# Longer rows for the windowed keys: four heads to a key tile, with row groups exchanged in the copies out of the transposes

## Chip, cores, metric

One core of one Trainium2 chip. The metric is the device time of one execution, in microseconds.

## The reference

Two attention blocks of one decode step, whose outputs stand side by side:

```python
# A: full attention.   B: the same, over the last W = 2048 positions only.
# 4 batches, 32 query heads, 8 key heads, 8192 positions, 128 elements a head, bf16
q = (x @ wq) -> [4, 32, 1, 128]
k = repeat(k_cache[:, :, Sk - W:, :], 4, axis=1)     # B; A takes the whole cache
v = repeat(v_cache[:, :, Sk - W:, :], 4, axis=1)
p = softmax(q @ k^T * 128 ** -0.5)
out = (p @ v) -> [4, 1, 4096] @ wo
```

Nearly all the bytes are keys and values: 134 MB of A, 33.6 MB of B, and 16.8 MB of weights.

## The kernel before

The work is cut into 20 units of 4 MB of keys and 4 MB of values. Units 0 to 3 are B, one batch each, all eight heads. Units 4 to 19 are A, two heads of one batch each. Keys and values each have two buffers of `[128 partitions, 128 token slots, 128]`. SyncE issues all the loads, in order, each behind the wait that its buffer is free.

```python
def kv_load(kind, u):                       # B units
    for q in range(NSEG):                   # NSEG = 4 pieces of 1 MB
        base = cache[un["b"], 2 * q, SK - W:SK, :]
        # TS = 32 tokens: rows of 8 KB; partition = 2 * run + head, two heads a piece
        src = bass.AP(..., ap=[[TS * DH, 64], [SK * DH, 2], [1, TS * DH]])
        w = [("T", tjob_idx[(u - 2, 4 * q + 3)])]       # keys: tile 4q+3 of the unit two before is transposed
        op("sp", dma(buf[:, slot, q * TS:(q + 1) * TS, :], src), waits=w, ...)
    # (A units: one DMA, [[NT * DH, 128], [1, NT * DH]], rows of 32 KB)

def pe_T(u, k):                             # tile k of 16: four transposes into one PSUM bank
    for pi in range(4):
        t0 = k * 8 + 2 * pi                 # two token slots each, as f32 pairs
        pe.transpose(out=bkf[:, pi * 128:(pi + 1) * 128], in_=K_sbf[:, slot, t0:t0 + 2, :], identity=identf)
    # copy PSUM -> SBUF: VectorE (as int32) for even k, ScalarE (as bf16) for odd k

def pe_S(u, k):                             # scores of tile k, three tiles after its transposes
    for pi in range(4):
        t = k * 8 + 2 * pi
        for e in range(2):                  # even and odd elements of the head
            pe.matmul(out=stb[:, t % NTH * C:(t % NTH + 2) * C], lhsT=ktv[:, pi, :, e],
                      rhs=RQc[:, u % 2, t // TS, e, :], start=(e == 0), stop=(e == 1))
```

A score row (one partition) gets columns for both heads of its piece; a mask by the partition's parity removes the wrong one. So exactly two heads may share a score tile, and the score of (partition, slot) must belong to the same token and head as the value at (partition, slot). That tied keys to the 8 KB rows of the values.

## Time and profile before

| | before |
|---|---|
| median of the first three runs | 440.12 us (439.64 to 440.31) |
| bytes, mean rate | 184.75 MB, 422 GB/s |
| rate while B loads / in the A stretch | 422 / 431 GB/s |
| busy: PE, DVE, ACT | 83%, 48%, 44% |

The page, the windows, the waits and two landings stand in the prediction. Two more views are needed to follow the change. The first is the page's list of transfers (KB each, median us from issue to landing):

```profile
K_sb<-in_B_k_cache_dram SPq DMA_DIRECT2D x16, 1024.0 KB, 22.0
V_sb<-in_B_v_cache_dram SPq DMA_DIRECT2D x16, 1024.0 KB, 18.4
```

A megabyte is 2.5 us of transfer at this rate, so of 22 us nearly 20 are time spent in the queue. The second is the groups of ScalarE and of VectorE by form between 34 and 124 us (count, busy us, mean ns, idle before), the copies out of the transposes:

```profile
L288 ACT ACTIVATE KT_sb<-KT 128x1024 bf16<-128x1024 bf16 x40 | 40.7, 1025 | 25.3 <-PE KT L279 25.3
L287 DVE COPY KT_sb<-KT 128x512 int32<-128x512 int32 x40 | 27.6, 690 | 36.8 <-PE KT L279 36.5
```

ScalarE waits 25.3 us for PE beside 40.7 of copying, VectorE 36.5 beside 27.6; in the same window no wait of PE for either of them is listed, so neither holds PE up.

### The profile page before, as it was taken

How to read it: one execution, taken by the hardware profiler on the slowest of the kernel's cores; microseconds unless marked ns; L12 is line 12 of the kernel's file. 1: busy time of each engine (PE TensorE's matmuls, PEld its weight loads, DVE VectorE, ACT ScalarE, POOL GpSimd, SP SyncE). 2: the span in 40 equal slices, each digit the busy share in tenths (PEclk: the TensorE clock that was granted, in tenths of full speed). 3: DMA queues.
4: the chain of work that ended last, by engine and by line, in shares of the span. 5: the costliest groups of instructions: out<-in, count | busy, mean ns of one | idle time of the engine just before them, and what ended most of it. 6: DMA issues, size and time to landing. Idle time of an engine off the chain costs nothing.

```text
span 437.9 us, 15510 instructions
## 1 busy us (share of the span) xinstructions
PE 363.9 (83%) x7174; PEld 336.5 (77%) x7184; DVE 209.5 (48%) x404; ACT 193.3 (44%) x217; POOL 29.1 (7%) x96
## 2 busy tenths in 40 slices
PE   0078898998998959896989598969878895989986
PEld 0068897997997959795979588968868795979975
DVE  0004455664565634463456247625644563556641
ACT  1033473563653625372635264534534361635630
POOL 7110000000000000000000000000100000000000
PEclk9999999999999997999899699989998999999999
DMA  8999999999999999999999999999999999999996
GB/s 336 431 412 418 419 419 419 421 445 406 450 431 431 417 445 431 434 428 431 434 434 428 432 434 431 428 434 431 406 456 431 431 428 434 431 431 410 446 407 253
DMA packets 12500, 184.75 MB, mean 422 GB/s; under 512 B 1428, under 2 KB 2504, under 8 KB 2760
## 3 DMA queue, kind: packets, MB, share of 16 engines
q1 hardware_dynamic: 12400, 184.56, 99.2%
q8 instruction: 8, 0.13, 0.1%
q14 instruction: 4, 0.03, 0.0%
q0 software_dynamic: 64, 0.02, 0.0%
q10 hardware_dynamic: 24, 0.01, 0.0%
HBM read 184.56 MB, written 0.01 MB: 421 GB/s over the span
## 4 chain that ended last, share of the span: by engine, by line
PE 51%; DMA 43%; issue 2%; DVE 1%; SPq 1%; PEld 1%; PEldq 0%
DMA K_sb<-in_A_k_cache_dram 29%; PE KT L279 25%; PE OT L326 10%; DMA K_sb<-in_B_k_cache_dram 7%; DMA V_sb<-in_A_v_cache_dram 7%; PE SB L310 4%; PE SA L310 4%; PE KT L384 4%; SPq L568 1%; PE SA L338 1%; DVE oacc L392 1%; PE KT L326 1%; PEld OT L326 1%; PE KT L262 0%; DVE OS L489 0%
## 5 line engine op out<-in xcount | busy, mean ns | idle before, releaser
L279 PE MATMUL KT<-identf,K_sb 128*128 128x128 f32 x1280 | 206.2, 294 | 44.0 <-DMA K_sb<-in_A_k_cache_dram 33.0
L288 ACT ACTIVATE KT_sb<-KT 128x1024 bf16<-128x1024 bf16 x160 | 163.4, 1025 | 121.1 <-PE KT L279 121.1
L279 PEld LDWEIGHTS KT<-identf,K_sb 128*128 128x128 f32 x1280 | 146.2, 148 | 49.4 <-DMA K_sb<-in_A_k_cache_dram 34.2
L287 DVE COPY KT_sb<-KT 128x512 int32<-128x512 int32 x160 | 110.5, 690 | 131.2 <-PE KT L279 129.9
L326 PE MATMUL OT<-PT,V_sb 128*128 128x64 bf16 x2560 | 78.1, 193 | 2.5 <-issue 1.4
L326 PEld LDWEIGHTS OT<-PT,V_sb 128*128 128x128 bf16 x2560 | 75.9, 98 | 2.7 <-issue 1.5
L457 ACT ACTIVATE PT<-Dt 128x512 bf16<-128x512 f32 x40 | 24.6, 632 | 84.1 <-DVE Dt L446 84.1
L310 PEld LDWEIGHTS SA<-RQc,KT_sb 128*128 128x128 bf16 x1280 | 56.7, 98 | 2.3
L310 PEld LDWEIGHTS SB<-RQc,KT_sb 128*128 128x128 bf16 x1280 | 51.1, 97 | 7.9 <-issue 4.4
L310 PE MATMUL SA<-RQc,KT_sb 128*128 128x16 bf16 x1280 | 56.2, 170 | 0.0
L310 PE MATMUL SB<-RQc,KT_sb 128*128 128x16 bf16 x1280 | 52.8, 170 | 0.0
L408 DVE TENSOR_REDUCE M<-SB 128x8 f32<-128x512 f32 (+1 forms) x20 | 13.8, 692 | 49.9 <-PE SB L310 49.9
L429 POOL PARTITION_ALL_REDUCE MB<-M1m x20 | 7.7, 387 | 333.3 <-DVE M1m L422 333.3
L384 PE MATMUL KT<-Wo_sb,OL 128*4 128x512 bf16 x80 | 18.9, 379 | 0.0
L200 PE MATMUL KT<-ident,x_sb 4*128 4x4 bf16 x8 | 0.6, 170 | 21.1 <-POOL identf L540 21.1
L200 PEld LDWEIGHTS KT<-ident,x_sb 4*128 4x128 bf16 x8 | 0.4, 113 | 21.3 <-issue 21.3
L464 DVE TENSOR_REDUCE LB<-SA 128x8 f32<-128x512 f32 (+1 forms) x20 | 13.7, 684 | 2.8 <-PE SA L338 2.8
L446 DVE TENSOR_TENSOR Dt<-SA,MBm 128x512 f32<-128x512 f32 x20 | 13.8, 692 | 0.7
L355 DVE TENSOR_TENSOR ORx<-KT,MSK 32x1024 bf16<-32x1024 bf16 x10 | 12.1, 1211 | 3.7 <-PE KT L350 3.7
L408 DVE TENSOR_REDUCE M<-SA 128x8 f32<-128x512 f32 (+1 forms) x20 | 13.6, 681 | 0.0
L446 DVE TENSOR_TENSOR Dt<-SB,MBm 128x512 f32<-128x512 f32 x20 | 13.6, 681 | 0.0
L338 PE MATMUL SA<-PT,onesb 128*128 128x128 bf16 x168 | 12.7, 218 | 0.0
(74 smaller groups left out, 119.7 us busy)
## 6 DMA issues: line engine op xcount, KB each, us to landing
K_sb<-in_A_k_cache_dram SPq DMA_DIRECT2D x15, 4096.0 KB, 22.6
V_sb<-in_A_v_cache_dram SPq DMA_DIRECT2D x15, 4096.0 KB, 30.6
K_sb<-in_B_k_cache_dram SPq DMA_DIRECT2D x16, 1024.0 KB, 22.0
V_sb<-in_B_v_cache_dram SPq DMA_DIRECT2D x16, 1024.0 KB, 18.4
V_sb<-in_B_wq_dram SPq DMA_DIRECT2D x1, 4096.0 KB, 12.5
V_sb<-in_A_wq_dram SPq DMA_DIRECT2D x1, 4096.0 KB, 22.0
Wo_sb<-in_B_wo_dram SPq DMA_DIRECT2D x4, 1024.0 KB, 11.9
K_sb<-in_A_k_cache_dram SPq DMA_DIRECT2D x2, 2048.0 KB, 18.9
```

What stands on the lines that cost most here:

```text
L279: ins = pe.transpose(out=bkf[:, pi * 128:(pi + 1) * 128], in_=K_sbf[:, slot, t0:t0 + 2, :].rearrange("p t d -> p (t d)"), identity=identf[ ...
L287: return e.tensor_copy(out=KT_sb.bitcast(I32)[:, tj % NKT, :], in_=bkf.bitcast(I32)[:, :])
L288: return e.activation(out=KT_sb[:, tj % NKT, :], in_=bk[:, :], func=ACTF.Copy)
L310: ins = pe.matmul(out=stb[:, t % NTH * C:(t % NTH + 2) * C], lhsT=ktv[:, pi, :, e], rhs=RQc[:, u % 2, t // TS, e, :], start=(e == 0), stop ...
L326: ins = pe.matmul(out=otb[:, s * NW:s * NW + w], lhsT=V_sb[:, slot, t, :], rhs=PT[:, slot, t * C:t * C + w], start=(j == 0), stop=(j == n ...
L338: ins = pe.matmul(out=SA[u % 2][:, s * NM:(s + 1) * NM], lhsT=onesb[:, :], rhs=PT[:, u % 2, c0:c0 + NM], start=(i == 0), stop=(i == n - 1))
L355: return dve.tensor_tensor(out=ORx[:, :, :, :], in0=bk[0:NR, 0:128].rearrange("p (i o r) -> p r o i", o=1, r=C).broadcast_to([NR, C, C, 12 ...
L384: ins = pe.matmul(out=bk[0:Bn, 0:D], lhsT=OL[:, i, :], rhs=Wo_sb[:, i, :], start=(i == 0), stop=(i == C - 1))
L408: return dve.tensor_reduce(out=M1[:, h * n:(h + 1) * n].rearrange("p (s h) -> p s h", h=C), in_=bank[:, :].rearrange("p (s j h) -> p s h j ...
L446: return dve.tensor_tensor(out=Dt[:, h * NTH * C:(h + 1) * NTH * C].rearrange("p (s j h) -> p s j h", s=Sh, h=C), in0=bank[:, :].rearrange ...
L457: return act.activation(out=PT[:, u % 2, a:b], in_=Dt[:, a:b], func=ACTF.Exp, scale=scale)
L464: return dve.tensor_reduce(out=LB[:, 0:n].rearrange("p (s h) -> p s h", h=C), in_=SA[u % 2][:, 0:NSEG * NM].rearrange("p (s j h) -> p s h ...
```

## The change

The intent: keys of B in rows of 16 KB, so in half as many packets. A row of 16 KB is 64 tokens, a piece then has 32 runs of four heads, and the transposed tile holds four heads. The copy out of PSUM, which the kernel before has too, exchanges groups of rows so that each score tile again holds two heads, in the layout of the values.

```diff
+    NPART = {"K": 2, "V": NSEG}
+        def tok0(k, pi):
+            return NTH * (k // (NJ // 2)) + TS * (pi // 2) + 4 * (k % (NJ // 2)) + 2 * (pi % 2)
 # pe_T and pe_S
-                    t0 = k * 8 + 2 * pi
+                    t0 = tok0(k, pi)
 # the copy
-                if eng == "dve":
-                    return e.tensor_copy(out=KT_sb.bitcast(I32)[:, tj % NKT, :], in_=bkf.bitcast(I32)[:, :])
-                return e.activation(out=KT_sb[:, tj % NKT, :], in_=bk[:, :], func=ACTF.Copy)
+                parts = [(dst, sr)]
+                if units[u]["P"] == 1:
+                    z = 2 if eng == "dve" else 4
+                    dv = dst.rearrange("p (b y a z) -> p b y a z", b=2, a=2, z=z)
+                    sv = sr.rearrange("p (a y b z) -> p b y a z", a=2, b=2, z=z)
+                    parts = [(dv[:, b, :, :, :], sv[:, b, :, :, :]) for b in range(2)] if eng != "dve" else [(dv, sv)]
+                for d, r in parts:
+                    ins = e.tensor_copy(out=d, in_=r) if eng == "dve" else e.activation(out=d, in_=r, func=ACTF.Copy)
 # kv_load, B units
-                for q in range(NSEG):
-                    base = cache[un["b"], 2 * q, SK - W:SK, :]
-                    src = bass.AP(..., offset=base.offset, ap=[[TS * DH, 64], [SK * DH, 2], [1, TS * DH]])
+                base = cache[un["b"], 0, SK - W:SK, :]
+                hw = SK * DH
+                n = NT // NPART[kind]
+                for q in range(NPART[kind]):
-                        w = [("T", tjob_idx[(u - 2, 4 * q + 3)])] if u >= 2 else []
+                        w = [("T", tjob_idx[(u - 2, 8 * q + 7)])] if u >= 2 else []
+                    heads = HKV // NPART[kind]
+                    src = bass.AP(..., offset=base.offset + q * heads * hw, ap=[[n * DH, W // n], [hw, heads], [1, n * DH]])
 # A units: the semaphore bump that stands for the missing pieces
-            op("sp", lambda sp: sp.sem_inc(sem, 48), waits=w, bump=(sem, 48, None))
+            bump = 16 * (NPART[kind] - 1)
+            op("sp", lambda sp: sp.sem_inc(sem, bump), waits=w, bump=(sem, bump, None))
```

Why the exchange is right: before the copy, column (a, y, b, z) of a tile comes from token block a and from row group y of four partitions, half b. The copy writes it to (b, y, a, z). So block a becomes part of the partition, and the pair of heads b becomes part of the slot: partition 4y + 2a + (p mod 2), head pair b. That is the values' layout, partition = 2 x run + head.

More of the change, by code (lines that the diff above doesn't have):

```diff
@@ L285, in efn @@
             def efn(e):
-                if eng == "dve":
-                    return e.tensor_copy(out=KT_sb.bitcast(I32)[:, tj % NKT, :], in_=bkf.bitcast(I32)[:, :])
-                return e.activation(out=KT_sb[:, tj % NKT, :], in_=bk[:, :], func=ACTF.Copy)
+                dst, sr = (KT_sb.bitcast(I32), bkf.bitcast(I32)) if eng == "dve" else (KT_sb, bk)
+                dst, sr = dst[:, tj % NKT, :], sr[:, :]
+                parts = [(dst, sr)]
[6 more added lines that the diff above has]
+                    ins = e.tensor_copy(out=d, in_=r) if eng == "dve" else e.activation(out=d, in_=r, func=ACTF.Copy)
+                return ins
             return dict(eng=eng, fn=efn, waits=[("T", idx)], inc=("E", idx))
@@ L307, in fn @@
                 for pi in range(4):
-                    t = k * 8 + 2 * pi
+                    t = tok0(k, pi)
                     for e in range(2):
@@ L717, in kv_load @@
             if un["P"] == 1:
-                for q in range(NSEG):
-                    base = cache[un["b"], 2 * q, SK - W:SK, :]
-                    src = bass.AP(tensor=base.tensor, offset=base.offset, ap=[[TS * DH, 64], [SK * DH, 2], [1, TS * DH]])
+                base = cache[un["b"], 0, SK - W:SK, :]
+                hw = SK * DH
+                n = NT // NPART[kind]
+                for q in range(NPART[kind]):
                     if kind == "K":
-                        w = [("T", tjob_idx[(u - 2, 4 * q + 3)])] if u >= 2 else []
+                        w = [("T", tjob_idx[(u - 2, 8 * q + 7)])] if u >= 2 else []
                     else:
                         w = [("otr", u - 2)] if u >= 2 else [("T", tjob_idx[(1, 1)])] if u else [("T", qp_idx[(1, NQP - 1)])]
-                    op("sp", dma(buf[:, slot, q * TS:(q + 1) * TS, :], src), waits=w, inc=(kind if q == NSEG - 1 else kind + "h", u, q))
+                    heads = HKV // NPART[kind]
+                    src = bass.AP(tensor=base.tensor, offset=base.offset + q * heads * hw, ap=[[n * DH, W // n], [hw, heads], [1, n * DH]])
+                    op("sp", dma(buf[:, slot, q * n:(q + 1) * n, :], src), waits=w, inc=(kind if q == NPART[kind] - 1 else kind + "h", u, q))
                 return
@@ L770, in full @@
             if key[0] in ("K", "V") and len(key) == 2:
-                return (key[0], key[1], NSEG - 1 if units[key[1]]["P"] == 1 else 0)
+                return (key[0], key[1], NPART[key[0]] - 1 if units[key[1]]["P"] == 1 else 0)
             if key[0] == "F":
```

## The prediction

The sum came to 439.4 us: 440.1 less 0.7 for 4 x 18 packets of 10 ns on each engine. The cost of one more ScalarE start, from the trace's 632 and 1025 ns: at most 0.24 us a tile, so 8 x 0.24 = 1.9 us a unit and 7.6 in four. A tile's copies are then at most 1.03 + 0.24, about 1.26 us, where PE makes two tiles in 1.35 and reaches the scores three tiles, 2.0 us, later. Also cut are the grounds for 690 ns with exchanged reads (until the result that was the author's estimate), the size of the loss in the second rival, and a ceiling of the rate; at the 431 GB/s of the A stretch the 40 us of B keys would be 38.9.

> **What bounds the kernel now.** I read the page first, for the busy shares and the DMA row; then a table by windows, to set the stage that the change touches against the rest; then, transfer by transfer, when each was issued and when it landed; last the waits.
>
> The page of the kernel before:
>
> ```profile
> span 437.9 us, 15510 instructions
> PE 363.9 (83%) x7174; PEld 336.5 (77%) x7184; DVE 209.5 (48%) x404; ACT 193.3 (44%) x217; POOL 29.1 (7%) x96
> DMA  8999999999999999999999999999999999999996
> DMA packets 12500, 184.75 MB, mean 422 GB/s; under 512 B 1428, under 2 KB 2504, under 8 KB 2760
> ```
>
> The DMA row is full in 38 of 40 slices, while no engine is. 184.75 MB have to come in, and the work after the last of them is a short tail.
>
> The table by windows (columns: window, PE, PEld, DVE, ACT, POOL busy us with counts, clock, DMA share, GB/s); the first window is the stage in which B keys and values load, the second a long stretch of A units:
>
> ```profile
> 34.10:113.70 79.60, 75.30 (x1435) 70.12 (x1437) 43.51 (x77) 41.22 (x44) 3.12 (x10) 1.00 1.01 422
> 164.80:390.00 225.20, 194.72 (x3711) 180.68 (x3716) 114.82 (x223) 103.53 (x110) 10.47 (x38) 0.94 1.00 431
> ```
>
> The DMA share is 1.00 or 1.01 in both, so the transfers are never out of work, yet the B stage moves 2% fewer bytes a second. B units load rows of 8 KB (32 tokens of 256 B), 512 to a unit; A units rows of 32 KB, 128 to a unit. PE is 95% busy in the B stage, so it has to be asked whether PE, not DMA, sets the pace there. The chain that ended last does run through PE from 34 to 142 us. But it counts a transfer from its issue, queueing included, and that misleads. What decides is whether the queue ever runs dry. Transfers of a B unit of keys, the last of four pieces, and the A keys with the least room:
>
> ```profile
> L568 SPq DMA_DIRECT2D K_sb<-in_B_k_cache_dram x1: 535/535/535, 47.6 to 47.6; - x1
> DMA to landing us min/median/max: 16.7/16.7/16.7
> ...
> L568 SPq DMA_DIRECT2D K_sb<-in_A_k_cache_dram x1: 328/328/328, 124.8 to 124.8; - x1
> DMA to landing us min/median/max: 18.1/18.1/18.1
> ```
>
> A 1 MB piece takes about 2.5 us of transfer and a 4 MB unit about 9.7, so 14.2 us and 8.4 us of these times were spent behind other transfers. I made this list for every issue of the kernel: V of unit 1 is issued at 55.7 us while keys ahead of it land until 64.3 (8.6 us of work queued), keys of unit 6 at 124.8 while values ahead land until 133.2 (8.4 us). Every other issue has about as much or more. So from the first microseconds to the last value block the transfer engines work without a gap, and the kernel lasts as long as its bytes take, plus a start and a tail. The waits agree: PE's only large wait for anything in the steady state is for keys,
>
> ```profile
> PE KT L279 <- DMA K_sb<-in_A_k_cache_dram: 33.0, 10, 5.3
> ```
>
> and nothing above a few us waits for the evictions of DVE or ACT.
>
> [...]
>
> **The change part by part.**
>
> *Transfers.* Only keys of the four B units change: 4 x 4 MB of the 184.75. Rows fall from 512 to 256 a unit, so 32 to 16 for each of 16 engines; issues fall from four to two, so two completion packets fewer per engine. That is 18 packets fewer per engine and unit. The cost of one packet comes from the landings. B: 44.0 us (keys of unit 1 in) to 113.7 (values of unit 3 in) less 9.7 us for the A keys among them leaves 60.0 us for six units, 10.0 each. A: from 196.4 to 235.3 four units landed, 9.73 each. The difference, 0.27 us, stands for 27 packets per engine (32 + 4 against 8 + 1): 10 ns each.[...] With 10 ns: 18 x 10 ns = 0.18 us a unit, **0.7 us for four units**[...]. Since the queue is never empty, all of that reaches the end.
>
> *Copies on ACT.* Each of 32 odd tiles of B units becomes two instructions of 512 elements. [...]the trace's exponentials of 512 elements take 632 ns, so at worst 2 x 632 - 1025 = 0.24 us.[...] In the loop PE takes 0.49 + 0.18 us a tile in its chain, so an odd tile comes every 1.35 us[...]. On the end path: 0.
>
> *Copies on DVE.* Same 32 instructions of 512 int32, with pairs exchanged by the read pattern. I expect 690 ns still. On the path: 0.
>
> *PE, loads and waits.* The order of instructions on PE is the same; transposes read other token blocks of the same size, scores write other columns. The bump of the key semaphore for A units falls from 48 to 16, no time. Keys of units 2 and 3 are issued at tiles 7 and 15 of the unit two before instead of 3, 7, 11, 15. In unit 0 tile 7 lies at 41.8 us, when the queue has work until 54.4; tile 15 at 47.6, when the first half ends near 59. It costs nothing. Keys of unit 0 land about 0.2 us earlier (part of the 0.7).
>
> Sum: 440.1 - 0.7 = **439.4 us**.
>
> **Rivals.** (1) *Evictions slow PE in the B stage.* PE has 16.5 to 18 us of work a unit against 20.0 us of transfers, and lags at first. Were each of four units stretched by the full 1.9 us of ACT, later issues would come up to 7.6 us late, still under the smallest queue of 8.4 us. It would show as PE waits for ACT, and the end would not move; only with a DVE copy much slower than 690 ns as well would the queue drain, at 1 to 3 us: about 442.[...] (2) *Four heads at 2 MB pitch in one transfer collide in HBM.*[...] Against it: two heads at this pitch run at 420 now[...]. I give a visible loss 2%. (3) *The 2% deficit of the B stage is not rows but place or phase.* Wo pieces, also in 8 KB rows but in one block, land in 2.4 to 2.5 us, hardly slower than 32 KB rows, and the early wq load, with 32 KB rows, ran at 420 GB/s. Then the gain is 0, and the time 440.1. (4) *The gain is larger:* if longer rows reach the full 431 GB/s at once, 4 x 0.27 = 1.1 us, 439.0.
>
> **Range and chances.** The runs of before spread over 0.67 us. Gains of 0 to 1.1 us with that spread give 438.6 to 440.3. A change of over 2% would need 8.8 us; faster is out of reach, since keys of B take 40 us in all[...]. Faster 0.01, same 0.97, slower 0.02.
>
> **What would show it.** Packets: 4 x 256 rows and 8 x 16 completions fewer, 12500 - 1024 - 128 = 11348, and under 512 B 1428 - 128 = 1300. The rate between 34 and 114 us up from 422 to about 425, and a unit of B keys landing in 9.8 us after the transfer ahead of it.[...] DVE copies at 690 in both forms. PE's waits on ACT or DVE still near zero, and every issue still several us ahead of the queue's end. The prediction is wrong if a B unit of keys takes more than 10 us, if the DMA share falls below 1 after 114 us, or if PE's delay in the B stage reaches the queue's 8.4 us.

## The result and the profile after

| | before | after |
|---|---|---|
| median | 439.69 us (439.59 to 440.31, 6 runs) | 439.30 us (439.03 to 439.48, 6 runs) |
| ratio, 95% interval | | 0.9987 (0.9974 to 1.0) |
| packets | 12500 | 11348 |
| rate from 34 to 114 us | 422 GB/s | 426 GB/s |

A ratio here and below is the mean time of one kernel's fast runs over that of the other's of the same rounds, so not quite the ratio of the medians. 0.13% of 439.7 is 0.57 us: the time is the same by the 2% rule. The answering lines of the page after:

```profile
span 437.7 us, 15534 instructions
PE 365.7 (84%) x7174; PEld 338.4 (77%) x7184; DVE 209.5 (48%) x404; ACT 194.9 (45%) x249; POOL 29.0 (7%) x96
DMA  8999999999999999999999999999999999999996
DMA packets 11348, 184.75 MB, mean 422 GB/s; under 512 B 1300, under 2 KB 2376, under 8 KB 2632
```

The packets are exactly the 1024 rows and 128 completions fewer that were counted out. The DMA row is as full as it was. Windows, as before:

```profile
34.10:113.70 79.60, 75.65 (x1450) 70.53 (x1453) 44.28 (x78) 43.42 (x76) 3.10 (x10) 1.00 1.01 426
164.80:390.00 225.20, 196.31 (x3699) 182.25 (x3703) 114.57 (x222) 102.67 (x109) 10.42 (x38) 0.93 1.00 431
```

The B stage moves 4 GB/s more, the A stretch as before. The last key piece of unit 2 and the keys of unit 6 (issue, and time to landing):

```profile
L580 SPq DMA_DIRECT2D K_sb<-in_B_k_cache_dram x1: 534/534/534, 47.1 to 47.1; - x1
DMA to landing us min/median/max: 16.7/16.7/16.7
...
L580 SPq DMA_DIRECT2D K_sb<-in_A_k_cache_dram x1: 328/328/328, 123.9 to 123.9; - x1
DMA to landing us min/median/max: 18.5/18.5/18.5
```

Values of unit 4, the transfer ahead of the second of these, land at 132.7 us, so it was issued 8.8 us before its turn. Following landings: values of unit 3 come in at 113.2 instead of 113.7, values of unit 9 at 234.8 instead of 235.3, the last whole value block at 422.3 instead of 422.6. About half a microsecond is won by the end of the B stage and still there at 235 us; of this pair of profiled executions 0.3 us are left at the last block. The means of the six runs differ by 0.57. The copies by form in the window of before:

```profile
L299 ACT ACTIVATE KT_sb<-KT 128x512 bf16<-128x512 bf16 x64 | 34.4, 596 | 17.7 <-PE KT L283 17.7
L299 ACT ACTIVATE KT_sb<-KT 128x1024 bf16<-128x1024 bf16 x8 | 8.2, 1023 | 5.1 <-PE KT L283 5.1
L299 DVE COPY KT_sb<-KT 128x512 int32<-128x512 int32 x40 | 27.6, 690 | 36.6 <-PE KT L283 36.2
```

VectorE reads the exchanged groups at the old speed, 690 ns a tile. On ScalarE 64 halves keep it busy 34.4 us, 0.54 us each although one lasts 0.596: the second half starts before the first has ended. A tile costs 1.08 us instead of 1.02.

### The profile page after: what moved, and what is told of

The parts are those of the page before. It is cut to its first block, busy times and chain, and to the rows that moved or that the text cites. A ratio compares the mean times of both kernels' runs of the same rounds, so it can differ in the third digit from the quotient of the medians.

```text
span 437.7 us, 15534 instructions
## 1 busy us (share of the span) xinstructions
PE 365.7 (84%) x7174; PEld 338.4 (77%) x7184; DVE 209.5 (48%) x404; ACT 194.9 (45%) x249; POOL 29.0 (7%) x96
## 2 busy tenths in 40 slices
DMA packets 11348, 184.75 MB, mean 422 GB/s; under 512 B 1300, under 2 KB 2376, under 8 KB 2632
## 4 chain that ended last, share of the span: by engine, by line
PE 51%; DMA 43%; issue 2%; DVE 1%; SPq 1%; PEld 1%; ACT 0%; PEldq 0%
DMA K_sb<-in_A_k_cache_dram 29%; PE KT L283 25%; PE OT L338 10%; DMA K_sb<-in_B_k_cache_dram 7%; DMA V_sb<-in_A_v_cache_dram 7%; PE SB L322 4%; PE SA L322 4%; PE KT L396 4%; PE SA L350 1%; SPq L580 1%; DVE oacc L404 1%; PE KT L338 1%; PEld OT L338 1%; ACT KT_sb L299 0%; PE KT L263 0%
## 5 line engine op out<-in xcount | busy, mean ns | idle before, releaser
L299 ACT ACTIVATE KT_sb<-KT 128x1024 bf16<-128x1024 bf16 (+1 forms) x192 | 165.0, 881 | 119.8 <-PE KT L283 119.8
L283 PEld LDWEIGHTS KT<-identf,K_sb 128*128 128x128 f32 x1280 | 148.0, 150 | 48.1 <-DMA K_sb<-in_A_k_cache_dram 31.4
```

Source lines behind the costliest of these rows:

```text
L283: ins = pe.transpose(out=bkf[:, pi * 128:(pi + 1) * 128], in_=K_sbf[:, slot, t0:t0 + 2, :].rearrange("p t d -> p (t d)"), identity=identf[ ...
L299: ins = e.tensor_copy(out=d, in_=r) if eng == "dve" else e.activation(out=d, in_=r, func=ACTF.Copy)
```

## The experiments

The result is as small as the noise of single runs, so it cannot explain itself. The theory to test: the time is bytes plus a fixed cost for each packet on each transfer engine, and nothing that PE, VectorE or ScalarE do in the B stage reaches the end. Rivals: the B stage is slow for its place or phase; the gain comes from the new placement or waits; four heads 2 MB apart cost HBM bandwidth; the split copies take something back. "Per engine" below means one sixteenth of the packets.

**The change once more, on another chip visit.**

> The changed kernel once more, on the chip of the three runs beside it. My theory (10 ns for each row or completion packet saved on each transfer engine, 18 of them per unit, four units, nothing else on the path): 0.5 to 0.7 us under the kernel before. The rival that the shortfall of the B stage belongs to the place or the phase and not to the row length: equal to before within 0.2 us.

Measured: 439.09 us against 439.76, ratio 0.999 (0.9977 to 1.0004), 427 GB/s in the B stage. The size is again about half a microsecond (0.44 by the ratio); the interval alone would not exclude none.

**Rows cut in two, everything else kept.**

```diff
-  src = bass.AP(..., ap=[[n * DH, W // n], [hw, heads], [1, n * DH]])
+  for h in range(2):       # keys only: two issues of rows half as long, to the same places
+      src = bass.AP(..., offset=... + h * m * DH, ap=[[n * DH, W // n], [hw, heads], [1, m * DH]])   # m = n // 2
```

> Changed kernel with one part undone: each 16 KB row of B keys is loaded as two 8 KB rows in two issues, to the same places; four heads a tile, exchanged copies and waits for tiles 7 and 15 all stay. Result correct. Row length theory: the gain goes, the time is that of the kernel before (0.0, within 0.2 us), 12500 packets again, B stage at 422 GB/s. If the gain came from the placement of four heads or from the later, fewer waits: stays 0.5 us under before.

Measured: 439.64 us, ratio 1.0001 (0.9988 to 1.0015); 12500 packets. The windows of this kernel, same columns:

```profile
34.10:113.70 79.60, 75.69 (x1458) 70.57 (x1461) 44.30 (x78) 43.80 (x77) 3.10 (x10) 1.00 1.02 423
```

The rate is back at 423, from 427 in the repeat of the change, and this goes with the rows, not with the four heads, the copies or the later waits. The times agree (1.0001 against 0.999), but their intervals overlap: that the time follows the rows rests on the doses below.

**Plain copies.**

```diff
-                if units[u]["P"] == 1:
+                if False:                # no exchange: a score tile holds four heads
```

> Changed kernel with the copies of the B units back to whole, unexchanged ones (wrong result on purpose: a score tile then holds four heads). My theory says that the split copies on ACT (about 1.4 us a unit) are hidden behind queued transfers: time as the changed kernel, within 0.2 us. Rival, that evictions in the B stage reach the end: up to 1.4 x 4 = 5.6 us faster than the changed kernel, at the least 0.5 us.

Measured: 439.71 us, ratio 0.9997 (0.9983 to 1.001), 427 GB/s in the B stage. By the means it is 0.35 us slower than the changed kernel of the same visit, within the noise, so the 0.2 us foretold cannot be checked; a gain of 0.5 us on it, the least of the rival, would be a ratio of 0.998, outside the interval. Taking the exchange away gains nothing that can be seen; the split copies are hidden. A warning came with it: the run was marked correct, though keys of four heads were taken for two. With these inputs the scores are tiny: the query elements are near 0.05 x 0.05 = 0.0025, a key element 0.05, so a scaled score is near 0.0025 x 0.05 = 1e-4 (an estimate from the inputs), and the softmax weights are equal to about that. The output hardly depends on the keys. So the correctness check cannot vouch for the exchange; the index argument above does.

**Dose: rows of 4, 8, 16 and 32 KB.** One run has all B loads in 4 KB rows (`NPART` 8 and 8, one head a piece), one has the keys of A cut down to 8 KB rows in the kernel before, one has all B loads in 32 KB rows over four heads, from a window of 4096 tokens.

> All B loads in 4 KB rows, one head to a piece, eight pieces of 512 KB a unit (wrong result on purpose). Row length theory: per engine and unit 64 rows and 8 completions against 32 and 4, 36 x 10 ns = 0.36 us, for eight loads 2.9 us over before; packets 12500 + 4096 + 512 = 17108. Place or phase rival: equal to before.

> Kernel before, with the keys of A units (all but the last) cut from 32 KB rows into four issues of 8 KB rows, same places, result correct. Here rows are short in another stage and in one block of memory, with no heads alternating. Row length theory: 15 loads of 24 rows and 3 completions more per engine at 10 ns, 4.1 us over before (about 444). Place or phase rival, that the B stage is slow for another reason: equal to before.

> All B loads in 32 KB rows as in the run that fell to 210 GB/s, but four heads at a time (from a window twice as long, so wrong data on purpose; same bytes). If eight heads 2 MB apart are what halves the rate[...]: full rate, 2.2 us under before. If the row length of 32 KB with strides does it: 80 us over, as the eight head run.

| run | packets per engine against before | ratio (95%) | difference | per packet |
|---|---|---|---|---|
| 4 KB rows, B | + 8 x 36 = 288 | 1.0054 (1.0038 to 1.0071) | + 2.4 us | 8.2 ns |
| 8 KB rows, keys of A | + 15 x 27 = 405 | 1.0074 (1.0057 to 1.009) | + 3.3 us | 8.0 ns |
| rows cut in two | 0 | 1.0001 | 0.0 | |
| the change | - 4 x 18 = 72 | 0.9987 (0.9974 to 1.0) | - 0.57 us | 7.9 ns |
| 32 KB rows, B, four heads | - 8 x 27 = 216 | 0.9962 (0.9945 to 0.9979) | - 1.7 us | 7.7 ns |

The difference is the ratio's distance from 1 times 439.8 us. Two stages, two directions, one head or four, correct and wrong data: always about 8 ns. They agree more closely than their intervals warrant: the tightest, with the keys of A, allows 6.2 to 9.8 ns, the change by itself 0 to 16. The 10 ns of the expectations lies just outside the tightest. The rival of place or phase falls, above all with the keys of A. There only the rows and the number of issues were changed, and the windows show the drop where the shortened rows are (first the B stage, then the A stretch; 431 before):

```profile
34.10:113.70 79.60, 75.43 (x1458) 70.35 (x1461) 44.30 (x78) 41.81 (x45) 3.12 (x10) 1.00 1.01 420
164.80:390.00 225.20, 192.95 (x3606) 178.92 (x3612) 112.03 (x215) 102.30 (x108) 10.11 (x37) 0.93 1.01 425
```

And with 32 KB rows the B stage runs at the A rate:

```profile
34.10:113.70 79.60, 75.76 (x1444) 70.58 (x1446) 43.91 (x77) 43.42 (x76) 3.10 (x10) 1.00 1.01 431
```

**Eight heads: a cliff.** Before the last of those runs I had tried 32 KB rows the natural way, all eight heads of the true window in one transfer:

```diff
-    NPART = {"K": 2, "V": NSEG}
+    NPART = {"K": 1, "V": 1}        # ap = [[128 * DH, 16], [hw, 8], [1, 128 * DH]]
     # (the wait for the key buffer and the semaphore bump are fitted to one piece)
```

> All B loads, keys and values, in 32 KB rows over eight heads, one issue a unit (wrong result on purpose; the work of every engine is the same). Row length theory: eight loads each save 24 rows and 3 completions per engine at 10 ns, 2.2 us under before, and the B stage runs at the 431 GB/s of A units although eight heads lie 2 MB apart. Pitch rival: eight heads at 2 MB cost bandwidth, no faster than before. Place or phase rival: equal to before, B stage at 422.

Measured: 519.76 us, ratio 1.1824 (1.1808 to 1.184), 80 us slower. The windows show where:

```profile
34.10:113.70 79.60, 52.11 (x842) 48.60 (x843) 24.27 (x42) 26.26 (x50) 1.57 (x5) 0.87 1.00 213
```

213 GB/s, half of the usual rate, and yet a DMA share of 1.00: all the engines have a packet in hand all the time, and each takes twice as long (in the packet records of the traces a packet of 32 KB takes 2.54 us between 40 and 100 us here, by the median, and 1.22 us in the A stretch of the kernel before). My first reading was HBM, as in the rival of the prediction: heads a power of two apart. So I changed the pitch:

```diff
-                hw = SK * DH
+                hw = SK * DH - 16 * DH      # 4 KB short of 2 MB
```

> As the eight head run with 32 KB rows, but with a head pitch 4 KB short of 2 MB (wrong data on purpose). If it is the power of two in the pitch that halves the rate: full or nearly full rate, about 2 us under before. If it is the number of heads or the order of rows, whatever the pitch: 80 us over, as the eight head run.

Measured: 520.15 us, ratio 1.1828 (1.1808 to 1.1847). The power of two in the pitch is not it. The four head run above has the same 32 KB rows and the same 2 MB pitch and is fast, so neither is row length. What is left that differs in the loads is the shape of the source: 16 groups of eight rows against 32 of four. The next run keeps the shape and drops the heads (210 to 215 GB/s is what it foretold if the shape is the cause):

```diff
-  ap=[[n * DH, W // n], [hw, heads], [1, n * DH]]
+  ap=[[9 * n * DH, 16], [n * DH, 8], [1, n * DH]]     # eight neighbouring rows, one row skipped, 16 times
```

> The 32 KB rows once more, but all eight rows of a group lie one after another in one head and the 16 groups 288 KB apart: no heads, no 2 MB steps (wrong data on purpose). The source's outermost dimension is still 16[...].[...] 210 to 215 GB/s in the B stage and about 80 us over before, as the two eight head runs. HBM theory (heads far apart are slow): full rate, 1.6 us under before.

Measured: 519.03 us, ratio 1.1815 (1.178 to 1.185):

```profile
34.10:113.70 79.60, 53.74 (x863) 50.16 (x863) 25.29 (x43) 27.06 (x52) 1.58 (x5) 0.87 1.00 217
```

Rows next to each other in memory, and still half the rate. The HBM theories, of heads and of their pitch, fall; the outermost count of 16, with eight rows in each, does it: 213 and 217 GB/s, against 431 with 32 groups of four rows of the same length. Why this shape costs half is not shown: the packet records name neither the engine nor where a packet is written. The A units, with 128 rows of 32 KB in one dimension, ran at 431.

**Runs outermost.** The change puts the runs, not the heads, in the outermost place. What does that save?

```diff
-  ap=[[n * DH, W // n], [hw, heads], [1, n * DH]]
+  ap=[[hw, heads], [n * DH, W // n], [1, n * DH]]     # keys only
```

> Changed kernel with the four heads outermost in the transfers of B keys and the runs inside (wrong order on purpose): the alternative that the change avoids. [...]4 of 16 carry all B keys: about 4.2 MB more or less on each of them over 12 that idle, 550 us[...]. If the split does not follow that dimension: as the changed kernel.

Measured: 622.25 us, ratio 1.4155 (1.4126 to 1.4183), 72 us over the 550 foretold. The windows:

```profile
34.10:113.70 79.60, 18.03 (x340) 17.18 (x340) 9.78 (x16) 9.91 (x18) 0.70 (x2) 0.96 0.43 114
34.10:45.00 10.90, 0.00 (x0) 0.00 (x0) 0.00 (x0) 0.00 (x0) 0.00 (x0) 1.00 0.25 60
```

Here the DMA share itself falls, to 0.43 with some value loads in the window and to 0.25 where only keys are under way (second line), and PE waits 179.5 us for B keys. The packet records show exactly four packets in hand there: with the share of 0.25, four of the 16 engines carry the load while the others idle, as many as there are heads in the outermost place. The same four engines move 60 GB/s in these 11 us and 109 GB/s between 97 and 105 us. The second is full speed for four (431 / 16 = 27 GB/s each, an estimate from the A stretch), the first only about half of it. Why is not shown; no run was made to test it.

**How much eviction the queue hides.** Two runs make the ScalarE copies of B units dearer, with right results:

```diff
+  if eng != "dve":
+      parts = [(d[:, c * y:(c + 1) * y, :, :], r[:, c * y:(c + 1) * y, :, :]) for d, r in parts for c in range(m)]   # y = 64 // m
+      # m = 2: four pieces a tile;  m = 4: eight
```

> Changed kernel with the ACT copies of B units in four pieces of 256 elements instead of two of 512 (result correct). Each piece costs a fixed start: halves took 596 ns against 1023 whole, so about 170 ns fixed; four take about 1.5 us, 0.17 over the 1.35 us in which PE makes two tiles, 1.4 us a unit. Theory that the queue of at least 8 us hides it: time as the changed kernel (0.5 us under before). Rival, evictions reach the end: 5 us over.

> The same with eight pieces of 128 elements: about 2.2 us a tile, 0.85 over PE's pace, 6.8 us a unit, 27 us in four. That is more than the queue holds, so here the end moves: about 27 - 8 = 19 us over before (10 to 25), and the transfers show gaps between 80 and 160 us. If the end does not move, my account of what hides the copies is wrong.

Measured: four pieces 439.53 us, ratio 1.0004 (0.9987 to 1.0021); eight pieces 440.45 us, ratio 1.002 (1.0003 to 1.0036). Four behave as foretold within the noise. Eight do not: 0.9 us over before instead of 19. ScalarE by form, between 34 and 124 us, with four pieces and with eight:

```profile
L301 ACT ACTIVATE KT_sb<-KT 128x256 bf16<-128x256 bf16 x128 | 38.3, 394 | 13.8 <-PE KT L283 11.5
```

```profile
L301 ACT ACTIVATE KT_sb<-KT 128x128 bf16<-128x128 bf16 x256 | 44.6, 431 | 11.9 <-PE KT L283 11.9
```

Eight pieces last 431 ns each by the mean but occupy 44.6 / 256 = 174 ns: several are under way at once. A tile takes 8 x 174 ns = 1.4 us, not 2.2, hardly over PE's 1.35. I had added up durations where only the distance of starts counts. PE's lag at the start of unit 4 is 1.8 us over the changed kernel (108.7 against 106.9 us in the chain), far less than the queue. So this run tests less than I meant it to: that the end would move once the lag passes some 8 us is not shown. Nor are the eight pieces' 1.4 us over the changed kernel explained in full. The landings differ by at most 0.5 us between 29 and 94 us, by 0.2 at 143 and by 0.8 at 153, with 16 packets in hand all the time, so it was no empty queue. The page offers a candidate: a queue that it calls instruction moves more here, where ScalarE has 192 more instructions. First the changed kernel, then eight pieces (packets, MB, share):

```profile
q14 instruction: 4, 0.03, 0.0%
q14 instruction: 6, 0.05, 0.0%
```

One of the six, of 8 KB, starts at 145.74 us in the packet records and lasts 0.31 us, and the 32 KB packet that starts as it ends lasts 1.59 us instead of 1.22. Together that is 0.69 us, as much as the landing at 153 us is late. No run tests this, and the rest stays open.

## Why the prediction was right

*What bounds the kernel.* Right, as far as tested. Every run above that moved the time by more than 1.4 us moved the transfers; those that added ScalarE work to every odd tile moved it by 1.4 us at the most. None of those made PE late by more than about 2 us, so the reserve of 8 us that the prediction counted on was not put to the test. The chain's PE stretch from 34 to 142 us, which the prediction set aside, was rightly set aside.

*The gain per packet.* The term was 18 packets, four units, 10 ns: 0.7 us. The count was exact. The cost is about 8 ns, by the dose runs, so 0.58 us; measured were 0.57 and 0.44, neither of them clear of noise alone. My 10 came from one odd transfer. Of the six units that I averaged to 10.0 us, the values of unit 0 landed 10.37 us after the transfer ahead, the other five 9.90 to 9.94, 9.92 by the mean. Against 9.72 in the A stretch that is 0.20 us for 27 packets, 7.6 ns: the better figure stood in the same trace. Why that one took longer is not shown.

*A unit of B keys in 9.8 us.* Right, but not so cleanly. Landing to landing, keys of unit 2 took 10.03 us and those of unit 3 9.79 (before 9.93 and 9.94). The prediction had called itself wrong if such a unit took more than 10 us; by the letter this sign was met once, by 0.03 us. In the four other traces with this loading (the repeat, plain copies, four and eight pieces) seven of eight such units took 9.69 to 9.81 us and one 10.23, so it was too sharp a sign for one landing. Keys of unit 0, foretold 0.2 us earlier, came 0.04 us earlier, those of unit 1 0.20. From keys of unit 1 to values of unit 3 the time fell from 69.72 to 69.43 us (69.04 in the repeat).

*Copies.* Hidden, as said. The duration of a half, 596 ns, lay under the 632 ns of the worst case. The cost was far under it: up to 7.6 us of ScalarE, the page shows 1.6 (193.3 to 194.9), since the halves overlap. VectorE kept its 690 ns.

*Rivals.* Place or phase fell in the dose runs. Longer rows reaching the full 431 GB/s at once did not happen at 16 KB; it did at 32. The HBM collision did not occur: four heads 2 MB apart ran at 431 GB/s, and with eight, rows side by side in memory were as slow (217 against 213 GB/s). But a loss of half the rate did lie one step further on, for a reason that was in none of my rivals. The prediction judged the new access pattern by its addresses in memory alone; the count in its outermost place mattered more (16 groups of eight rows 213 to 217 GB/s, 32 of four 431), and that 32 was safe was luck: I had not checked it.

## What to carry to other kernels

When one queue of transfers is never empty, count its bytes and its packets and leave the engines alone (here dearer copies moved the time by 1.4 us at the most); a transfer's time from issue to landing can be mostly queue (here nearly 20 of 22 us), and a chain built on it points at the wrong engine. Lengthening rows paid about 8 ns for each packet saved on an engine, so multiply before building: here 1024 rows were half a microsecond, and all B loads at 32 KB would have been 1.7 us. Before loading rows in a new order, look at the outermost count of the access pattern: here 32 groups of four rows ran at 426 to 431 GB/s, 16 groups of eight at 213 to 217, and four groups of 32 on four engines alone, at 60 to 109.
